# Top-8 search over five interleaved segments instead of six contiguous ones, in a top-k attention and MLP kernel

## The chip, the cores and the metric

The kernel runs on one core of one Trainium2 chip. The core has five engines that work side by side and meet only through semaphores: TensorE (PE in the profile, with its weight loads as PEld), VectorE (DVE), ScalarE (ACT), GpSimd (POOL) and SyncE (SP), which issues most of the DMAs. The metric is the device time of one execution in microseconds (us), the median of several runs.

## What is computed

Sparse attention for 8 batches of 8 heads, 576 tokens, head size 64: each row of scores keeps only its 32 largest of 576 values, and a softmax over those weights the values. The result, 4608 tokens of 512 features, goes through a two-layer MLP with a leaky ReLU whose slope is given per hidden unit.

```python
scores = scale * np.matmul(q, k.transpose(0, 1, 3, 2))
kth = np.partition(scores, -top_k, axis=-1)[..., -top_k:-top_k + 1]     # top_k = 32
scores = np.where(scores >= kth, scores, -1000000000.0)
attn = np.exp(scores - np.max(scores, axis=-1, keepdims=True))
attn = attn / (np.sum(attn, axis=-1, keepdims=True) + 1e-09)
x = np.matmul(attn, v)                       # 8 x 8 x 576 x 64, then heads side by side
...
h = x @ w_in                                 # 512 -> 2048
g = np.maximum(h, 0.0) + alpha * np.minimum(h, 0.0)
return g @ w_out                             # 2048 -> 512
```

## The kernel before

**Tiles.** Two heads form a pair; there are 32 pairs. A tile is 128 rows of scores, 576 wide; a pair has nine, of which the ninth holds the 64 rows left over from each of its two heads. That makes 288 tiles of [128, 576].

**How the 32nd value is found.** For each row a threshold is guessed from the mean and the spread of its scores (`prep_plan`, once per pair: small matmuls on PE, `P` on DVE, then a short chain of DVE operations to `NT0`). ACT subtracts it: `b` is score minus guess. ACT then sums the signs of `b` into `S_all`, which tells how many of the row's scores lie above the guess, and so on which side the wanted value lies and how many places away. POOL makes the side into a sign bit, `SG`. DVE flips bits of `b` by it (`flip`, the tile `y`), so that the values on the wanted side nearest to the guess become the largest. Now only the 24 largest of `y` are needed, in order.

- `seg_ops` cuts the 576 values of `y` into NSEG segments and takes the eight largest of each with one DVE instruction (`nc.vector.max`, MAX8 in the profile). The results stand side by side in `C`, 8 NSEG values a row.
- `merge_ops` takes the 24 largest of those in three rounds into `L`: MAX8 over all of `C`, then a match-and-replace that strikes the eight out (two instructions in the profile, MATCH_VALUE_LOAD and MATCH_REPLACE8), twice over.
- `sel_a` (ACT), `sel_eq`, `sel_pr` and `sel_sum` (DVE, for three tiles at a time) pick the wanted one of the 24 into `KK`; `limit` turns it back into a limit `KP` for `b`.
- `check_group` keeps, once per nine tiles, the largest eighth value of any segment in `M8`. If a row's wanted value lies below it, one segment may have held more than eight candidates. At the end `checks` counts over all rows that this and three other conditions hold; if any fails, a flag sends the whole kernel through a slow second path (`general_batch`).

**After the limit.** DVE makes a 0/1 mask `mk` (`mask`), ACT the exponentials `e` for two tiles at once, POOL multiplies both into `w` (`weights`). A DMA transposes `w` to `wT`. PE multiplies it with the values into `pu` (`av`), which has a column of ones for the sum; DVE takes the reciprocal `rz`, ACT scales into `xb`. Further DMA transposes give `xT`, and PE and ACT run the MLP on it in blocks (`ph`, `gT`, `pz`, `o_sb`), with the second term of the leaky ReLU folded into the weights beforehand.

**What sets the order.** The order on each engine is written out by hand: the main loop goes through ticks n, and in each of them issues

- on PE the scores of the next unit of one or two tiles (two PSUM buffers), a slice of the MLP or of the weights' preparation, then the steps of `prep_plan` and `av` due in this tick;
- on ACT the evacuations left over from the tick before (`gT`, `o_sb`), then `b`, the sign sum and `e` of tile n, then what is due;
- on DVE first the mask of tile n - 7, then the search of tile n - 2 and the merge of tile n - 3, one instruction of each in turn, then what is due (the limits, the steps of `prep_plan`), then the flip of tile n - 1;
- on POOL first `w` of tile n - 7, which waits for the mask of this tick, then `SG` of tile n - 1, for which the flip at the end of this tick waits.

Each engine works through its own list in order, so an instruction that waits holds everything behind it on that engine. `b` has five buffers of two tiles, `e` four, `y` two, `C` two of nine tiles each. `P` is read by PE, and DVE reads its PSUM source from a pool of two banks that `pu` uses as well.

The lines to follow are 369 (the search), 384 and 386 (the merge), 359 (`y`), 433 (`mk`), 443 (`w`), 353 (`SG`), 246 (`P`), 337, 343 and 348 (`b`, the sign sum, `e`), 328 (scores), 494 (`pu`), 697, 703 and 715 (the MLP). The turn of search and merge in one tick is this:

```python
segs = seg_ops(n - LAG_S) if 0 <= n - LAG_S < NT else []
...
for i in range(max(len(segs), len(merges), 2)):
    if i < len(segs):
        segs[i]()
    if i < len(merges):
        merges[i]()
```

Of the kernel before, what the change touches and what calls it, by code (L numbers as in the profile page):

```python
# [14 lines left out]
PS = bass.MemoryType.PSUM  # L15

S = 576
NSEG = 6
SEG = S // NSEG
KW = 24  # L20
TINY = 1.0e-30
ZSQ = 0.640625
# [10 lines left out]
def kernel(  # L33
# [10 lines left out]
    nc = tc.nc  # L44
# [8 lines left out]
    TPP = 9  # L53
# [109 lines left out]
    n = 0  # L163
# [200 lines left out]
    def seg_ops(n):  # L364
        if n % TPP == 0:
            Cs[n // TPP] = prep.tile([128, TPP, NSEG, 8], FP32, name="C", bufs=2)
        C = Cs[n // TPP]
        t = tiles[n]
        return [lambda g=g: nc.vector.max(out=C[:, n % TPP, g, :],  # L369
                                          in_=t["y"][:, g * SEG:(g + 1) * SEG])  # L370
                for g in range(NSEG)]

    Ls, sel, KPs = {}, {}, {}

    def merge_ops(n):
# [3 lines left out]
        L = Ls[n // 3][:, n % 3, :]  # L379
        C2 = attn.tile([128, NSEG * 8], FP32, name="C2", bufs=1)  # L380
        ops = []
# [368 lines left out]
    with tc.manual_schedule(engines={E.PE, E.Activation, E.DVE, E.Pool, E.SP}):  # L750
# [84 lines left out]
        n = 0  # L835
        end = max(NT + 24, 0)
        while n < end or back or after:
# [55 lines left out]
            if 0 <= n - 1 < NT:  # L893
                side_of(n - 1)
            segs = seg_ops(n - LAG_S) if 0 <= n - LAG_S < NT else []
            mn = n - LAG_M
            merges = merge_ops(mn) if 0 <= mn < NT else []
# [167 lines left out]
```

## Time and profile before

| | us |
|---|---|
| median of 3 runs | 874.53 |
| lowest and highest run | 871.5, 876.87 |
| the profiled execution | 873.98 |
| its span, first to last instruction | 872.1 |
| mean granted TensorE clock in it | 0.943 |

The costliest groups of DVE and ACT, by line, operation, output and input (partitions x elements), count, then busy time and mean nanoseconds of one, then idle time of the engine just before them and what ended it:

```profile
L384 DVE MAX8 L<-C 128x8 f32<-128x48 f32 x864 | 162.6, 188 | 0.1
L359 DVE TENSOR_SCALAR y<-b,SG 128x576 int32<-128x576 int32 x288 | 147.0, 510 | 8.2 <-POOL SG L353 7.8
L433 DVE TENSOR_SCALAR mk<-b,KP 128x576 bf16<-128x576 f32 x282 | 143.6, 509 | 0.0
L386 DVE MATCH_REPLACE8 C<-L,C 128x48 f32<-128x48 f32 x576 | 108.3, 188 | 0.0
L337 ACT ACTIVATE b<-ps,NT 128x576 f32<-128x576 f32 x288 | 202.3, 761 | 3.1 <-PE ps L328 3.1
L343 ACT ACTIVATE h<-b 128x576 bf16<-128x576 f32 x288 | 202.9, 705 | 1.7
```

Successive instructions of one engine overlap in such a profile: the drawn time of one reaches into the next, so busy time of a group is more than the time it takes on its engine. The chain of waits gives each piece only the time by which it carries the chain on. Times in a trace count from the span's start.

### The profile page before, as it was taken

The numbers are of one execution on the slowest core, as the hardware profiler recorded it, in microseconds if no ns is written. First come the engines' busy times: TensorE is split into PE (matmuls) and PEld (weight loads), VectorE is DVE, ScalarE is ACT, GpSimd is POOL, SyncE is SP. The second block draws the span as 40 slices with busy tenths as digits, with TensorE's granted clock in tenths as the row PEclk, the third lists the DMA queues.
The fourth block names the chain that finished last, engine by engine and source line by source line (L and its number), as shares of the span: only waits on it lengthen the run. The fifth ranks groups of instructions, "written<-read, shape, count | busy, mean of one in ns | idle before, by whom it ended". The sixth has DMA issues, their size and how long they took to land.

```text
span 872.1 us, 20608 instructions
## 1 busy us (share of the span) xinstructions
PE 721.9 (83%) x5697; PEld 428.3 (49%) x5771; DVE 835.1 (96%) x5188; ACT 790.3 (91%) x1873; POOL 431.0 (49%) x630
## 2 busy tenths in 40 slices
PE   6776688778978789787987789977897988899996
PEld 4443444334554345444454445643455554566674
DVE  4999999999999999999999999999999999999992
ACT  6999999999999999889999999989999899979861
POOL 1455545555454555545555455554554555544530
PEclk9997779899979999989998999989999999999999
DMA  7999644644665545564576445475455543535442
GB/s 161 156 178 199 131 89 90 126 91 97 135 139 107 108 102 116 100 135 95 114 154 115 98 97 116 111 136 98 92 128 121 121 103 81 106 71 100 91 96 56
DMA packets 342619, 99.37 MB, mean 114 GB/s; under 512 B 334672, under 2 KB 334944, under 8 KB 342496
## 3 DMA queue, kind: packets, MB, share of 16 engines
q1 hardware_dynamic: 340144, 95.58, 54.4%
q0 software_dynamic: 1152, 2.10, 2.0%
q8 instruction: 47, 0.77, 0.4%
q14 instruction: 76, 0.62, 0.2%
q10 hardware_dynamic: 1200, 0.30, 0.2%
HBM read 36.71 MB, written 9.44 MB: 53 GB/s over the span
## 4 chain that ended last, share of the span: by engine, by line
DVE 62%; ACT 21%; PE 12%; DMA 2%; issue 1%; POOL 1%; SPq 0%; DVEq 0%; another core or an unknown queue 0%; ACTq 0%
DVE C L369 20%; DVE y L359 9%; DVE mk L433 9%; DVE C L386 8%; DVE L L384 7%; ACT b L337 5%; ACT h L343 5%; ACT e L348 4%; PE ps L328 4%; PE pz L715 3%; PE ph L697 2%; ACT gT L703 2%; DVE P L246 2%; ACT xb L523 2%; PE pu L494 1%
## 5 line engine op out<-in xcount | busy, mean ns | idle before, releaser
L443 POOL TENSOR_TENSOR w<-mk,e 128x576 bf16<-128x576 bf16 x250 | 319.3, 1277 | 337.9 <-DVE mk L433 187.5
L369 DVE MAX8 C<-y 128x8 f32<-128x96 f32 x1728 | 419.1, 243 | 0.1
L328 PE MATMUL ps<-qkT 64*128 64x288 f32 (+1 forms) x1280 | 256.5, 474 | 35.1 <-ACT b L337 34.6
L337 ACT ACTIVATE b<-ps,NT 128x576 f32<-128x576 f32 x288 | 202.3, 761 | 3.1 <-PE ps L328 3.1
L343 ACT ACTIVATE h<-b 128x576 bf16<-128x576 f32 x288 | 202.9, 705 | 1.7
L697 PE MATMUL ph<-xT,w_in_b 128*128 128x128 bf16 (+2 forms) x997 | 150.4, 292 | 40.8 <-ACT gT L703 33.6
L328 PEld LDWEIGHTS ps<-qkT 64*128 64x128 f32 (+1 forms) x1280 | 134.3, 194 | 97.6 <-ACT b L337 59.8
L348 ACT ACTIVATE e<-b 128x1152 bf16<-128x1152 f32 (+1 forms) x158 | 174.2, 1102 | 0.0
L384 DVE MAX8 L<-C 128x8 f32<-128x48 f32 x864 | 162.6, 188 | 0.1
L359 DVE TENSOR_SCALAR y<-b,SG 128x576 int32<-128x576 int32 x288 | 147.0, 510 | 8.2 <-POOL SG L353 7.8
L433 DVE TENSOR_SCALAR mk<-b,KP 128x576 bf16<-128x576 f32 x282 | 143.6, 509 | 0.0
L715 PE MATMUL pz<-w_out_b,gT 128*128 128x512 bf16 x543 | 132.4, 380 | 1.2 <-issue 0.5
L697 PEld LDWEIGHTS <-w_in_b 128*128 128x128 bf16 x1024 | 80.4, 100 | 104.0 <-issue 79.6
L703 ACT ACTIVATE gT<-ph 128x512 bf16<-128x512 f32 x140 | 86.0, 621 | 28.1 <-PE ph L697 28.1
L386 DVE MATCH_REPLACE8 C<-L,C 128x48 f32<-128x48 f32 x576 | 108.3, 188 | 0.0
L715 PEld LDWEIGHTS <-gT 128*128 128x128 bf16 x560 | 51.6, 98 | 68.5 <-issue 14.0
L494 PE MATMUL pu<-v_bf,wT 128*128 128x65 bf16 (+1 forms) x1600 | 69.4, 198 | 14.4 <-DMA wT<-w 6.9
L494 PEld LDWEIGHTS <-wT 128*128 128x128 bf16 (+1 forms) x1600 | 65.2, 103 | 25.6 <-issue 10.2
L353 POOL TENSOR_SCALAR SG<-S_all 128x1 int32<-128x1 f32 x288 | 65.3, 227 | 18.9 <-ACT h L343 18.8
L443 POOL TENSOR_TENSOR wm<-mk,e 128x576 bf16<-128x576 bf16 x32 | 40.8, 1276 | 49.9 <-DVE mk L433 45.6
L343 ACT ACTIVATION_READ_ACCUMULATOR h<-b 128x1 f32 x288 | 62.8, 218 | 0.0
L523 ACT ACTIVATE xb<-pu,rz 128x64 bf16<-128x64 f32 x224 | 54.5, 369 | 0.0
(113 smaller groups left out, 728.1 us busy)
## 6 DMA issues: line engine op xcount, KB each, us to landing
out_dram<-o_sb SPq DMA_DIRECT2D x34, 256.0 KB, 2.3
st_q<-in_q_dram SPq DMA_DIRECT2D x64, 128.0 KB, 2.8
st_v<-in_v_dram SPq DMA_DIRECT2D x64, 128.0 KB, 2.6
kst<-in_k_dram SPq DMA_DIRECT2D x62, 128.0 KB, 2.6
w_stage<-in_moe_w_out_dram SPq DMA_DIRECT2D x16, 256.0 KB, 3.1
w_in_b<-in_moe_w_in_dram POOLq DMA_DIRECT2D x8, 256.0 KB, 6.4
wT<-w SPq DMA_TRANSPOSE x128, 3.3
st_q<-in_q_dram SPq DMA_DIRECT2D x32, 32.0 KB, 2.5
```

Of the source, the lines that this page charges most:

```text
L328: nc.tensor.matmul(o_, l_, r_, start=True, stop=True)
L337: nc.scalar.activation(t["b"].rearrange("p (a c) -> p a c", a=2), t["ps"], AF.Identity, bias=NT0[:, p * TPP + j:p * TPP + j + 1], scale=ON ...
L343: nc.scalar.activation(h, tiles[n]["b"], AF.Sign, accum_out=S_all[:, n:n + 1])
L348: nc.scalar.activation(e, tiles[n0]["bu"], AF.Exp, scale=scl)
L359: nc.vector.tensor_scalar(t["y"].bitcast(I32), t["b"].bitcast(I32), FLIP, SG[:, n:n + 1], ALU.bitwise_xor, ALU.bitwise_xor)
L369: return [lambda g=g: nc.vector.max(out=C[:, n % TPP, g, :], in_=t["y"][:, g * SEG:(g + 1) * SEG]) for g in range(NSEG)]
L384: ops.append(lambda r=r, src=src: nc.vector.max(out=L[:, 8 * r:8 * r + 8], in_=src))
L386: ops.append(lambda r=r, src=src: nc.vector.match_replace(out=C2, in_to_replace=L[:, 8 * r:8 * r + 8], in_values=src, imm_value=NEG))
L433: nc.vector.tensor_scalar(t["mk"], t["b"], row_limit(n), None, ALU.is_ge)
L443: nc.gpsimd.tensor_tensor(dst, t["mk"], t["e"], ALU.mult)
L697: nc.tensor.matmul(hold[f][:, i, :], w_in_b[:, kk, (f + i) * 128:(f + i + 1) * 128], xT[:, kk, c0:c0 + tb], start=(kk == 0), stop=(kk == N ...
L715: nc.tensor.matmul(pz[0:m], hold["gT"][:, f, r0:r0 + m], w_out_b[:, f, :], start=False, stop=(f == NFT - 1))
```

## The change

The six segments of 96 neighbouring values become five. The 576 values of a row are taken as 72 runs of eight neighbours, and segment g is made of the runs g, g + 5, g + 10 and so on: segments 0 and 1 have 15 runs (120 values), segments 2, 3 and 4 have 14 (112 values). One MAX8 reads each segment, with an access pattern of runs of eight words 40 words apart. `C` holds 40 values a row instead of 48, and the merge, the check and the small tile that the merge works in follow from NSEG. All lines below the constants move up by one, and the search stays on line 369.

```diff
 S = 576
-NSEG = 6
-SEG = S // NSEG
+NSEG = 5
 KW = 24
...
         t = tiles[n]
-        return [lambda g=g: nc.vector.max(out=C[:, n % TPP, g, :],
-                                          in_=t["y"][:, g * SEG:(g + 1) * SEG])
+        y = t["y"].rearrange("p (t e) -> p t e", e=8)
+        return [lambda g=g: nc.vector.max(out=C[:, n % TPP, g, :], in_=y[:, g:S // 8:NSEG, :])
                 for g in range(NSEG)]
```

## The prediction

> **What bounds the kernel now.** I read the page first, then the chain of waits in order of time, then the table of stretches cut where that chain changes engine.
>
> ```profile
> PE 721.9 (83%) x5697; PEld 428.3 (49%) x5771; DVE 835.1 (96%) x5188; ACT 790.3 (91%) x1873; POOL 431.0 (49%) x630
> DVE 62%; ACT 21%; PE 12%; DMA 2%; issue 1%; POOL 1%; SPq 0%; DVEq 0%; another core or an unknown queue 0%; ACTq 0%
> ```
>
> The change acts on DVE, which is 96% busy and holds 62% of the chain. But ACT is 91% busy: the average says only that two engines are close. So I look at where the chain lies on DVE.
>
> ```profile
> 118.37 0.82 DVE P L246 x2
> ...
> 351.19 1.24 PE pu L494 x30
> ...
> 427.98 0.81 DVE P L246 x2
> ...
> 811.66 0.49 DVE y L359
> ...
> 854.57 0.19 PE ptot L481 x2
> ```
>
> From 118 to 351 us the chain is DVE alone, from 351 to 428 ACT and PE, from 428 to 646 DVE again, then ACT and PE until 812, and DVE until 855. Before 118 it changes hands often.
>
> ```profile
> 40.00:118.00 78.00, 54.58 (x335) 32.69 (x341) 75.22 (x472) 76.06 (x174) 42.69 (x61) 0.80 0.87 160
> 118.00:351.00 233.00, 193.74 (x1494) 109.30 (x1513) 232.63 (x1450) 222.47 (x542) 121.36 (x171) 0.95 0.55 110
> 428.00:646.00 218.00, 183.56 (x1450) 104.36 (x1472) 218.00 (x1360) 205.31 (x505) 113.74 (x160) 0.96 0.56 115
> ...
> 812.00:855.00 43.00, 42.20 (x463) 28.73 (x464) 42.39 (x235) 29.99 (x59) 16.17 (x22) 1.00 0.47 94
> ```
>
> The columns are stretch, length, then busy time of PE, weight load, DVE, ACT, POOL. In both long DVE stretches DVE has no gap (232.63 of 233.00; 218.00 of 218.00), and ACT is idle for 10.5 and 12.7 us. What matters is whether that idle time is ACT waiting for DVE, which would shrink with DVE, or something else.
>
> ```profile
> PE ph L697 <- ACT gT L703: 10.5, 15, 1.5
> ...
> PE pu L494 <- DVE P L246: 5.1, 5, 1.9
> ```
>
> These are PE's own waits from 118 to 352 us. The same view from 428 to 646 us has:
>
> ```profile
> PE pu L494 <- DVE P L246: 1.0, 1, 1.0
> ```
>
> And ACT's waits over the whole run:
>
> ```profile
> ACT gT L703 <- PE ph L697: 28.1, 30, 2.6
> ACT o_sb L720 <- PE pz L715: 25.8, 15, 4.6
> ```
>
> ACT waits for PE and PE for ACT; ACT's list names DVE nowhere. The only door by which DVE holds the pair back is PE waiting for a PSUM bank that DVE's P product still reads: 5.1 us in the first long stretch (1.9 of it the single wait at 351 us that the chain goes through), 1.0 us in the second. So ACT and PE are a closed loop that is nearly as slow as DVE by itself.
>
> **The change, part by part.** The price of one search instruction is its place in the chain, not its drawn length, since neighbours overlap.
>
> ```profile
> 641.72 0.17 DVE C L369
> 641.88 0.11 DVE L L384
> 641.99 0.15 DVE C L369
> 642.14 0.18 DVE C L386
> ...
> 643.20 0.16 DVE C L369
> ```
>
> One tile runs six such C searches of 96 elements (0.16 us each on average), three L searches of 48 (0.11) and two match-and-replace pairs of 48 (0.18). It goes from 641.72 to 643.36, 1.64 us. From 96 to 48 elements the place shrinks by 0.05 us, 1.04 ns an element, so a fixed 0.06 us is left per instruction.
>
> (1) Five segments, two of 120 and three of 112 elements, still read 576 elements together; one fixed part goes: -0.06 us per tile. (2) The three L searches and two replacements read 40 instead of 48 elements: 5 x 8 x 1.04 ns = -0.04 us. The two value loads stay. (3) The check over the eighth of each segment reads 45 instead of 54 elements, 32 times: 0.3 us in all, left out. No DMA, no queue entry and no wait on another engine is added or moved. The five searches and five merge steps alternate as before, one search between dependent merge steps; only the search behind the last L search is gone, and what reads L next comes after y. Sum: -0.10 us per tile, 288 tiles, 30 us of DVE work.
>
> (4) The new cost is the way of reading: runs of eight words, then a jump of 40. No search in the trace reads so. The nearest rows:
>
> ```profile
> L407 DVE TENSOR_REDUCE KK<-L 128x3 f32<-128x72 f32 x96 | 20.7, 216 | 0.1
> L461 DVE TENSOR_REDUCE M<-C 128x9 f32<-128x54 f32 x32 | 7.5, 235 | 0.0
> ```
>
> L407 reads 72 adjacent words, so at 1.04 ns its fixed part is 141 ns. L461 picks every eighth word: (235 - 141) / 54 = 1.74 ns an element, 0.70 more than an adjacent one. If only the first word after a jump pays, 72 x 0.70 ns = 0.05 us per tile and half the saving is gone; if every word pays, 576 x 0.70 = 0.40 us and DVE loses 0.30 per tile; if a jump is free, nothing. A gain I exclude: the words are as many and none is read faster than in turn. I take nothing, since seven of eight words follow their neighbour as in L407, and keep 0 to 0.05 for the range. [...]
>
> (5) What DVE then waits for. In each pass y needs SG from POOL, and POOL does SG behind w, which needs this pass's mask mk.
>
> ```profile
> 403.10 0.51 DVE L433 TENSOR_SCALAR mk<-b,KP 128x576 bf16<-128x576 f32 x1
> 403.70 1.27 POOL L443 TENSOR_TENSOR w<-mk,e 128x576 bf16<-128x576 bf16 x1 [2.09 <-DVE mk L433]
> 404.94 0.23 POOL L353 TENSOR_SCALAR SG<-S_all 128x1 int32<-128x1 f32 x1
> 405.02 0.24 DVE L369 MAX8 C<-y 128x8 f32<-128x96 f32 x1
> 405.20 0.52 DVE L359 TENSOR_SCALAR y<-b,SG 128x576 int32<-128x576 int32 x1
> ```
>
> SG ends at 405.17, y starts at 405.20: in this pass there is no slack, although no wait is drawn (the search's drawn end covers it). The pass in the middle of nine later ones:
>
> ```profile
> 520.18 0.23 POOL L353 TENSOR_SCALAR SG<-S_all 128x1 int32<-128x1 f32 x1
> ...
> 520.70 0.51 DVE L359 TENSOR_SCALAR y<-b,SG 128x576 int32<-128x576 int32 x1
> ```
>
> Here y comes 0.29 us after SG's end. Read so over the nine passes from 515.11 to 537.90 us, three have 0.03 to 0.05 us between SG's end and y, six have 0.14 to 0.95. So of 9 x 0.10 us only about 6 x 0.10 passes through: 0.07 us per tile while DVE sets the pace.
>
> **The sum, stretch by stretch.** The searches of each stretch, six a tile:
>
> ```profile
> 40.00:118.00 78.00, 39.15 (x161) 0.80 0.87 160
> 118.00:351.00 233.00, 118.02 (x486) 0.95 0.55 110
> 428.00:646.00 218.00, 110.33 (x456) 0.96 0.56 115
> 812.00:855.00 43.00, 17.64 (x72) 1.00 0.47 94
> ```
>
> Before 118: 27 tiles, but ACT is busy 76.06 of 78.00, so between nothing and 27 x 0.07 = 1.9; I take -0.7, as DVE holds 47 of these 118 us of the chain (62% of 872 less the three later stretches' 494). First long stretch: DVE would shed 81 x 0.07 = 5.7, but ACT and PE follow at once when PE's waits for DVE are used up: at least the 1.9 at 351 us, at most 5.1; middle 3.5. 351 to 428: nothing, ACT and PE. Second: DVE sheds 76 x 0.07 = 5.3, PE's wait is only 1.0; -0.5 (0 to 1.0). 646 to 812: nothing; the pair sets it, and an earlier DVE only waits longer for S_all. 812 to 855: twelve tiles, 0.8 on DVE, but PE is busy 42.20 of 43.00, so at most that; -0.6. Together -5.3, and between -2 and -9 at the ends. The profiled execution took 873.98 us (span 872.1, 1.9 around it; the median of the runs is 874.53): 873.98 - 5.3 = 868.7, with 865 to 872 for this case alone.
>
> **The rivals.**
>
> (A) ACT's idle time gives way too, so that DVE's gain comes through in all its stretches: (27 + 81 + 76 + 12) x 0.07 = 13.7: 860. Without the POOL limit, at 0.10, it would be 854. For it: ACT's 23 us of idle in those stretches is room enough. Against: that idle ends on PE, not on DVE.
>
> (B) Nothing comes of it: jumps cost 0.05 us per tile, which leaves 0.05, and the pair takes over after 2 us: 872, up to 875 with what runs scatter.
>
> (C) Slower by the way of reading: every word pays as in L461, DVE loses 0.30 us per tile in 288 tiles, and DVE sets the pace everywhere: 874 + 86 = 960. It decides from about 0.20 ns an element, where (4) eats the 0.10. Against: seven words of eight follow their neighbour. [...]
>
> (D) Slower by PE's clock: with ACT and PE setting the pace, PE's pauses move:
>
> ```profile
> 367.78 1.87 PE L697 MATMUL ph<-xT,w_in_b 128*128 128x512 bf16 x4 [2.19 <-DMA xT<-xb]
> 370.12 3.13 PE L328 MATMUL ps<-qkT 64*128 64x288 f32 x8
> ...
> 377.46 1.24 PE L328 MATMUL ps<-qkT 64*128 64x288 f32 x8
> ```
>
> After a pause of 2.19 us eight score products take 3.13 instead of 1.24: with the ph group, about 4 us are lost. Four more such pauses without a gain elsewhere would make 890. Fewer would add 4 each to the gain. [...]
>
> (E) The kernel does more than the change says: if one row has eight of the values ahead of its wanted one in a single segment, the flag sends the whole kernel through its slow second path, which alone adds over a millisecond of searches (320 tiles of 576 elements, seven passes at 0.66 us from the prices above). Worked out on the reference's inputs by the kernel's formulas, the wanted rank is at most 18 and no row has more than seven there.
>
> **How the numbers follow.** My forecast 0.50, A 0.30, B 0.10, C 0.04, D 0.05, E 0.01. About 1% is what a measurement of this kernel tells from no change; faster is below 865.8, 1% under the median. A lies there, and a fifth of the forecast's chance for a pair with a little more room: 0.40. The rest of the forecast and B stay within 1%: 0.50. C, D and E are slower: 0.10. The range for 8 in 10 leaves out C, D, E and A's end at 854: from 857 to 876.
>
> **What would show it.**
>
> ```profile
> L369 DVE MAX8 C<-y 128x8 f32<-128x96 f32 x1728 | 419.1, 243 | 0.1
> ```
>
> This group becomes x1440 at a mean of 243 + 19 x 1.04 = 263 ns; above 270 a jump has a price, near 343 it is C (115 x 0.70 more). L searches and replacements get 8 ns shorter. In the two long stretches DVE's busy share falls below 99% with waits of y on SG and of P on PE, and "PE pu <- DVE P" all but goes; the chain there turns to ACT and PE. If DVE is still without a gap and the time is near 860, the step that gave ACT and PE no room was wrong. If C searches cost as forecast and the time doesn't move, the pair was the bound before as well.

## The result, and the profile after

| | before | after |
|---|---|---|
| median of 14 runs each, us | 874.0 | 870.01 |
| lowest and highest run, us | 871.35, 877.89 | 866.45, 875.27 |
| profiled execution, us | 873.98 | 871.45 |
| its span, us | 872.1 | 869.6 |

The ratio after to before is 0.9959 [0.9943, 0.9976] (in brackets the 95% interval): faster by 4.0 us, and within 1%. The forecast was 868.7, in a range from 857 to 876.

The page of the changed kernel, busy time by engine and then the chain that ended last:

```profile
PE 714.7 (82%) x5697; PEld 424.1 (49%) x5771; DVE 814.2 (94%) x4900; ACT 789.5 (91%) x1873; POOL 431.1 (50%) x630
...
PE 15%; ACT 10%; DVE 1%; issue 0%; POOL 0%; DVEq 0%
```

DVE gave up 288 instructions and 20.9 us of drawn time; ACT did the same work as before. The chain could be followed back only over the last quarter of the span (the shares add to 26%), so of the long stretches it says nothing. For those, here is the table of stretches (length, then busy time of PE, weight load, DVE, ACT and POOL, then granted clock, DMA share and GB/s):

```profile
40.00:118.00 78.00, 50.17 (x328) 29.36 (x331) 71.37 (x429) 74.39 (x170) 40.85 (x59) 0.71 0.87 153
118.00:351.00 233.00, 193.40 (x1522) 109.49 (x1546) 231.24 (x1400) 222.35 (x544) 124.34 (x175) 0.96 0.57 114
...
428.00:646.00 218.00, 184.94 (x1464) 105.34 (x1483) 212.70 (x1290) 204.93 (x504) 114.49 (x161) 0.95 0.59 114
```

DVE now has gaps: 1.8 us in the first long stretch and 5.3 in the second, where it had 0.4 and none. The groups of DVE, shapes kept apart:

```profile
L369 DVE MAX8 C<-y 128x8 f32<-128x112 f32 x864 | 225.2, 261 | 0.0
L383 DVE MAX8 L<-C 128x8 f32<-128x40 f32 x864 | 155.7, 180 | 0.1
L369 DVE MAX8 C<-y 128x8 f32<-128x120 f32 x576 | 154.9, 269 | 0.1
L358 DVE TENSOR_SCALAR y<-b,SG 128x576 int32<-128x576 int32 x288 | 147.4, 512 | 11.2 <-POOL SG L352 8.6
...
L385 DVE MATCH_REPLACE8 C<-L,C 128x40 f32<-128x40 f32 x576 | 103.8, 180 | 0.0
L385 DVE MATCH_VALUE_LOAD C<-L,C 128x8 f32 x576 | 39.9, 69 | 0.1
L245 DVE TENSOR_TENSOR P<-pr,qkT 128x512 bf16<-128x512 f32 x32 | 22.0, 687 | 12.2 <-PE pr L237 12.0
```

The 1440 searches take (225.2 + 154.9) / 1440 = 264 ns each; 263 was forecast for free jumps, and L searches and replacements went from 188 to 180. The new idle time is that of P, which waits 12.0 us for PE (2.7 before). On PE's side, the waits of the whole run:

```profile
PE ph L696 <- ACT gT L702: 38.4, 51, 1.5
PE ps L327 <- ACT b L336: 36.5, 32, 2.9
PE pt L215 <- ACT qkT L211: 26.0, 26, 2.4
PE pu L493 <- DMA wT<-w: 11.1, 2, 5.7
```

PE waiting for P's bank, the door of the prediction, is in this list nowhere any more. PE waits for ACT, and DVE for PE.

What a tile costs is best read from the starts of y, once a tile. A pair has nine tiles, so that y's tenth start, less the first, is the time of one pair. In the timeline of before:

```profile
560.77 0.52 DVE L359 TENSOR_SCALAR y<-b,SG 128x576 int32<-128x576 int32 x1
...
586.42 0.52 DVE L359 TENSOR_SCALAR y<-b,SG 128x576 int32<-128x576 int32 x1
```

And of after, the same nine places in a pair, with all ten starts:

```profile
325.93 0.52 DVE L358 TENSOR_SCALAR y<-b,SG 128x576 int32<-128x576 int32 x1
328.62 0.50 DVE L358 TENSOR_SCALAR y<-b,SG 128x576 int32<-128x576 int32 x1
331.37 0.50 DVE L358 TENSOR_SCALAR y<-b,SG 128x576 int32<-128x576 int32 x1
333.98 0.50 DVE L358 TENSOR_SCALAR y<-b,SG 128x576 int32<-128x576 int32 x1
336.73 0.50 DVE L358 TENSOR_SCALAR y<-b,SG 128x576 int32<-128x576 int32 x1
339.74 0.52 DVE L358 TENSOR_SCALAR y<-b,SG 128x576 int32<-128x576 int32 x1
342.33 0.52 DVE L358 TENSOR_SCALAR y<-b,SG 128x576 int32<-128x576 int32 x1
344.88 0.52 DVE L358 TENSOR_SCALAR y<-b,SG 128x576 int32<-128x576 int32 x1
348.43 0.51 DVE L358 TENSOR_SCALAR y<-b,SG 128x576 int32<-128x576 int32 x1
350.96 0.52 DVE L358 TENSOR_SCALAR y<-b,SG 128x576 int32<-128x576 int32 x1
```

25.65 us before, 25.03 after: 0.62 less for nine tiles, 0.069 a tile. That is the pair when DVE waits for nothing. Not every pair is one: of the 24 pairs between tile 36 and tile 252 the median is 25.66 before and 25.31 after, because P then waits for PE (12 times, 12.0 us). Where the two traces drift apart is seen from the start of y for single tiles, after less before:

| tile | before, us | after, us | after - before |
|---|---|---|---|
| 27 | 94.10 | 97.97 | +3.87 |
| 36 | 121.71 | 123.12 | +1.41 |
| 117 | 353.78 | 350.96 | -2.82 |
| 126 | 379.43 | 376.00 | -3.43 |
| 144 | 431.30 | 429.13 | -2.17 |
| 198 | 586.42 | 582.49 | -3.93 |
| 216 | 637.72 | 635.77 | -1.95 |
| 279 | 819.99 | 818.01 | -1.98 |
| 287 | 842.47 | 839.86 | -2.61 |

Nearly 4 us are lost up to tile 27, of which 2.5 are made good by tile 36. The first long stretch makes the rest good and gains, and in the second the gain is won and lost again.

### The profile page after: what moved, and what is told of

Same layout as the page of the kernel before. It is cut to its first block, busy times and chain, and to the rows that moved or that the text cites. A ratio compares the mean times of both kernels' runs of the same rounds, so it can differ in the third digit from the quotient of the medians.

```text
span 869.6 us, 20320 instructions
## 1 busy us (share of the span) xinstructions
PE 714.7 (82%) x5697; PEld 424.1 (49%) x5771; DVE 814.2 (94%) x4900; ACT 789.5 (91%) x1873; POOL 431.1 (50%) x630
## 5 line engine op out<-in xcount | busy, mean ns | idle before, releaser
L369 DVE MAX8 C<-y 128x8 f32<-128x112 f32 (+1 forms) x1440 | 380.0, 264 | 0.1
L327 PE MATMUL ps<-qkT 64*128 64x288 f32 (+1 forms) x1280 | 252.8, 467 | 36.9 <-ACT b L336 36.5
L696 PE MATMUL ph<-xT,w_in_b 128*128 128x128 bf16 (+2 forms) x997 | 151.2, 293 | 41.6 <-ACT gT L702 38.4
L327 PEld LDWEIGHTS ps<-qkT 64*128 64x128 f32 (+1 forms) x1280 | 131.2, 190 | 97.7 <-ACT b L336 60.8
L358 DVE TENSOR_SCALAR y<-b,SG 128x576 int32<-128x576 int32 x288 | 147.4, 512 | 11.2 <-POOL SG L352 8.6
L383 DVE MAX8 L<-C 128x8 f32<-128x40 f32 x864 | 155.7, 180 | 0.1
L702 ACT ACTIVATE gT<-ph 128x512 bf16<-128x512 f32 x140 | 85.9, 621 | 26.4 <-PE ph L696 26.2
L385 DVE MATCH_REPLACE8 C<-L,C 128x40 f32<-128x40 f32 x576 | 103.8, 180 | 0.0
L352 POOL TENSOR_SCALAR SG<-S_all 128x1 int32<-128x1 f32 x288 | 65.2, 227 | 22.0 <-ACT h L342 21.8
```

The costliest lines, as they stand in the source:

```text
L327: nc.tensor.matmul(o_, l_, r_, start=True, stop=True)
L358: nc.vector.tensor_scalar(t["y"].bitcast(I32), t["b"].bitcast(I32), FLIP, SG[:, n:n + 1], ALU.bitwise_xor, ALU.bitwise_xor)
L369: return [lambda g=g: nc.vector.max(out=C[:, n % TPP, g, :], in_=y[:, g:S // 8:NSEG, :]) for g in range(NSEG)]
L383: ops.append(lambda r=r, src=src: nc.vector.max(out=L[:, 8 * r:8 * r + 8], in_=src))
L696: nc.tensor.matmul(hold[f][:, i, :], w_in_b[:, kk, (f + i) * 128:(f + i + 1) * 128], xT[:, kk, c0:c0 + tb], start=(kk == 0), stop=(kk == N ...
```

## The experiments

The theory, from the prediction: the search as changed is cheaper by 0.10 us a tile, jumps are free, POOL's loop from mask to sign holds three of nine passes, and the time follows little because ACT and PE are nearly as slow by themselves. The rivals: the jumps cost what the saved instruction gave; the POOL loop is the limit; or no second limit is there, and the gain is only small.

### Do the jumps cost anything?

Six segments again, but of runs of eight with jumps of 48 words: one line of the changed kernel is edited, and against before nothing but the way of reading differs:

```diff
-NSEG = 5
+NSEG = 6
```

> Six segments again, but read as runs of eight words with jumps of 48 (the new way of reading alone, 96 elements as before). Theory (jumps are free): the search's mean stays at 243 ns within 2, and the time is that of the kernel before, ratio 0.998 to 1.002. Rival (jumps have a price that ate part of the saving): at 0.70 ns for the first word after each jump the search's mean is 251 ns, DVE loses 0.05 us per tile where it sets the pace, and the time is 8 to 14 us above the kernel before.

Measured: 873.95, ratio 1.0006 [0.9986, 1.0026]. The groups:

```profile
L369 DVE MAX8 C<-y 128x8 f32<-128x96 f32 x1728 | 426.2, 247 | 0.1
L383 DVE MAX8 L<-C 128x8 f32<-128x48 f32 x864 | 166.3, 192 | 0.1
```

The search is drawn 4 ns longer than before's 243, more than I had allowed. But the L search, whose reading isn't changed, is drawn 4 ns longer too (192 for 188): searches and merges are drawn some 2% longer in this profile. Drawn lengths move so without any jump too: in a later kernel with before's own search (the square on POOL, below) the two are drawn at 240 and 186. The place in the queue decides, and nine passes take 25.64 us (y at 560.71 and 586.35), as before, where a price of 0.05 us a tile would have made 0.45 more. These jumps cost nothing that shows here.

The other way round, five segments of neighbours, with the widths of the changed kernel (the edit is shown against that kernel):

```diff
+CUT = [0, 120, 240, 352, 464, 576]
...
-        y = t["y"].rearrange("p (t e) -> p t e", e=8)
-        return [lambda g=g: nc.vector.max(out=C[:, n % TPP, g, :], in_=y[:, g:S // 8:NSEG, :])
+        return [lambda g=g: nc.vector.max(out=C[:, n % TPP, g, :],
+                                          in_=t["y"][:, CUT[g]:CUT[g + 1]])
```

> Five segments of neighbours (120, 120, 112, 112, 112 values): the change without its jumps. Theory: the same lengths as in the changed kernel (mean 264 ns) and the same time, 868 to 872, ratio about 0.996. Rival (jumps have a price): the mean is 8 to 11 ns shorter and DVE has more room; since ACT and PE set the pace the time would still gain little, so the length of the search tells these apart, not the time.

Measured: 870.37, ratio 0.9968 [0.9948, 0.9988], the changed kernel's within the interval.

```profile
L369 DVE MAX8 C<-y 128x8 f32<-128x112 f32 x864 | 228.0, 264 | 0.0
...
L369 DVE MAX8 C<-y 128x8 f32<-128x120 f32 x576 | 156.6, 272 | 0.1
```

Neighbours are drawn no shorter than runs with jumps (261 and 269 in the changed kernel), and a quick pair takes 25.02 us. For the time it is the number of segments that counts; interleaving does nothing (870.37 without it, 870.01 with it).

### Does the time follow DVE any further down?

Four segments (the count in the flag's test is set so that it never strikes):

```diff
-NSEG = 5
+NSEG = 4
...
-        nc.vector.tensor_scalar(bad, pt, float(128 * NT * 4) - 0.5, None, ALU.is_lt)
+        nc.vector.tensor_scalar(bad, pt, -0.5, None, ALU.is_lt)
```

> Four segments of 144 values, merged from 32; the final check's flag is never raised (that decision is left out, the check's own work stays). DVE sheds another 0.10 us of work per tile. Theory (since the change ACT and PE set the pace): 867 to 871, at most 2 us below the changed kernel, and DVE's waits for PE and POOL grow by about what it sheds, some 20 us. Rival (DVE still sets the pace in the changed kernel): as much again as the change was to bring with DVE as the only bound, 0.07 us in each of some 200 tiles, so 856 or less.

Measured: 870.51, ratio 0.9954 [0.9937, 0.9972]. The time is that of the theory, but this run shows nothing, since DVE was not made quicker: nine passes take 25.15 us at best. The reason stands in the merge's group:

```profile
L383 DVE MAX8 L<-C 128x8 f32<-128x32 f32 x864 | 157.9, 183 | 10.0
```

10.0 us of idle time before the L searches, 0.1 in the changed kernel. Four searches no longer stand between all of the five merge steps, and the last L search, which needs the replacement just ahead of it, waits for it with nothing between:

```profile
411.68 0.17 DVE L385 MATCH_REPLACE8 C<-L,C 128x32 f32<-128x32 f32 x1
411.88 0.20 DVE L383 MAX8 L<-C 128x8 f32<-128x32 f32 x1
```

From the start of that replacement to the next instruction it is 0.20 us; with a search between, in the changed kernel, it is 0.10. That 0.10 a tile is what four segments in place of five were to save.

So the search was cut without touching the merge: five segments, but they read only the first half of each row (and the flag never strikes, as above). What this kernel leaves out is the candidates in the second half.

```diff
-        return [lambda g=g: nc.vector.max(out=C[:, n % TPP, g, :], in_=y[:, g:S // 8:NSEG, :])
+        return [lambda g=g: nc.vector.max(out=C[:, n % TPP, g, :], in_=y[:, g:S // 16:NSEG, :])
```

> The changed kernel with its five searches reading only the first half of each row (288 of 576 values, five searches of 56 or 64); the second half of the candidates is left out, and the final check's flag is never raised. Unlike with four segments, the five searches still stand between the merge steps. DVE's own work falls by 288 x 1.04 ns = 0.30 us per tile, but POOL's loop (mask, w, SG, y) floors a pass: nine passes should go from 25.0 to about 24.4 us where nothing else waits. Theory (ACT and PE set the pace of the changed kernel): 866 to 871, less than 4 us below it, and DVE waits 10 us or more longer for PE and POOL. Rival (DVE, with POOL's loop, still sets the pace): 0.07 us per tile more is gained, 15 us, 856 or less.

Measured: 870.31, ratio 0.9957 [0.9941, 0.9974]: no quicker than the changed kernel, with 288 x 288 elements less to read, 86 us of DVE work at 1.04 ns. DVE's waits over the whole run, and the long stretches:

```profile
DVE y L358 <- POOL SG L352: 32.4, 104, 3.3
DVE P L245 <- PE pr L237: 22.8, 19, 2.6
```

```profile
118.00:351.00 233.00, 195.85 (x1544) 110.23 (x1543) 217.03 (x1396) 221.30 (x541) 124.06 (x174) 0.95 0.57 113
428.00:646.00 218.00, 187.82 (x1485) 106.68 (x1483) 201.92 (x1302) 208.22 (x511) 115.84 (x163) 0.95 0.59 116
```

DVE stands idle for 16 us in each long stretch, and ACT is busy as before. What the search gives up now turns into waits for POOL and PE. Something else sets the pace, and the changed kernel stands already at the point where it does. POOL's loop is not enough to explain it: seven of the 27 pairs from tile 36 on take 24.50 to 24.52 us, so the loop allows that, and still the 27 together take 693.3 us, against 694.9 in the changed kernel.

In the other direction, the kernel before with a seventh, short search:

```diff
-                for g in range(NSEG)]
+                for g in range(NSEG)] + [lambda: nc.vector.max(out=spare, in_=t["y"][:, 0:40])]
```

> The kernel before with one more search per tile, of 40 values into a tile that nobody reads: 0.06 + 0.04 = 0.10 us more on DVE per tile, the size of what the change takes off. Theory (DVE set the pace of the kernel before almost from end to end, with ACT and PE just behind): adding costs nearly in full, 0.10 us in some 230 to 288 tiles, 895 to 902, five times what taking off the same brought. Rival (ACT and PE were the bound before the change too, DVE merely full beside them): less than 8 us, below 882.

Measured: 895.18, ratio 1.0244 [1.0216, 1.0272]. Nine passes take 26.50 us (0.85 more, 0.094 a tile), DVE has no gap in the long stretches (233.00 of 233.00, 218.00 of 218.00), it holds 78% of the chain, and the door opens wide:

```profile
PE pu L495 <- DVE P L246: 19.1, 13, 2.9
```

0.09 us a tile added cost 21 us; 0.07 to 0.10 taken off gave 4. On the side of more work DVE decides (21 us are 0.073 for each of 288 tiles); on the side of less it doesn't.

### Is it POOL's loop?

The sign of tile n - 1 ahead of w in POOL's list, in the changed kernel:

```diff
             held = []
+            if 0 <= n - 1 < NT:
+                side_of(n - 1)
             for wn in due:
...
-            if 0 <= n - 1 < NT:
-                side_of(n - 1)
```

> The changed kernel with POOL doing SG ahead of w in each pass, so that y no longer waits behind the mask and w. Theory: the three passes of nine that kept their length (2.53, 2.59 and 3.01 us) get 0.05 to 0.10 us shorter, the quickest nine passes go from 25.0 to about 24.7 us, which shows that POOL's loop held them; the time stays within 868 to 873, since ACT and PE set the pace. Rival (those passes were held by something else): nine passes stay at 25.0.

Measured: 870.99, ratio 0.9953 [0.9931, 0.9975]. The three passes that kept their length under the change (3.01, 2.59 and 2.53 us) now take 2.92, 2.47 and 2.41, and the quickest pair takes 24.66 in place of 25.03. So POOL's loop did hold them, and the time is the same 870 with the loop open.

But the edit has a price of its own. In POOL's list w now stands behind a sign that waits for ACT, 207.8 us here and 21.8 in the changed kernel:

```profile
L352 POOL TENSOR_SCALAR SG<-S_all 128x1 int32<-128x1 f32 x288 | 90.0, 313 | 208.6 <-ACT h L342 207.8 <-DMA wT<-w 0.5
```

Where w comes late by that, it meets DVE's EQ or y, and these then last until w is done:

```profile
211.97 0.23 POOL L352 TENSOR_SCALAR SG<-S_all 128x1 int32<-128x1 f32 x1 [2.40 <-ACT h L342]
...
212.16 1.28 POOL L442 TENSOR_TENSOR w<-mk,e 128x576 bf16<-128x576 bf16 x1
...
212.52 1.01 DVE L396 TENSOR_TENSOR EQ<-ra,iota 128x72 f32<-128x72 f32 x1
```

In this profile 15 of the 96 EQ overlap w and take 723 ns in the mean (210 where POOL does nothing), and 13 y overlap it and take 947 (511). So this run alone doesn't tell what an open loop is worth; together with the half search, which left POOL's list as it was, it speaks against the loop as what sets the time. That POOL waits 207.8 us for ACT already points to ACT.

### Is it ACT?

If ACT and PE set the pace, then with less on ACT the change should be worth more. Two steps were moved from ACT to POOL, each in both kernels. First the cast of the values, for all pairs from the third on:

```diff
+        def pool_v():
+            nc.gpsimd.tensor_copy(d["v"][:, :, 0:D], d["st_v"])
...
-            ts = [-14, -13, -12, -11, -10, -9, -7, -6, -5, -5, -4, -4, -3, -2, -8]
+            ts = [-14, -13, -12, -11, -10, -9, -7, -6, -5, -5, -4, -4, -3, -2, -9]
...
-                 dict(dve=[dve_6]), dict(act=[act_v])]
+                 dict(dve=[dve_6]),
+                 dict(act=[act_v]) if p < 2 else dict(pool=[pool_v])]
...
                 side_of(n - 1)
+            run(n, "pool")
```

> The kernel before with one step taken off ACT: the cast of a pair's values to bf16 (0.73 us drawn, 30 of 32 pairs) goes to POOL's idle time behind SG in the pass with the most slack. ACT sheds about 19 us. Theory (DVE set the pace before): nine passes of DVE stay at 25.65 and the time falls by at most 4 us, 870 to 874. Rival (ACT was the bound before as well): 860 or less.

> The same step taken off ACT in the changed kernel. Theory (ACT and PE set the pace now, and DVE could do nine passes in 25.0 us): the pair's floor falls below DVE's, DVE runs without gaps from about 120 to 740 us, some 10 us are gained: 857 to 864, so that the change is worth 9 us or more with ACT relieved, against 4 without. Rival (PE, not ACT, is what DVE now waits for): 867 to 871.

Measured: before 884.62, ratio 1.0116 [1.0087, 1.0145]; after 870.46, ratio 0.996 [0.9945, 0.9976]. Both missed their forecasts (870 to 874 and 857 to 864), and the second lies where its rival said, 867 to 871, though not for the rival's reason. The cause is a collision that I had not thought of, in the timeline of the second:

```profile
528.58 0.72 POOL L205 CAST v_bf<-st_v 128x640 bf16<-128x640 f32 x1
...
528.62 0.69 DVE L246 TENSOR_TENSOR km<-GK,bones 128x2 bf16<-128x2 bf16 x1
```

km, a product of two elements a partition, ends with POOL's cast, 0.69 us after its start. Over the run it takes 584 ns in this kernel and 142 in the changed one. So each pair costs DVE half a microsecond more: nine passes take 26.10 us with six segments and 25.58 with five. In both DVE has next to no gap left (218.00 and 217.51 of 218.00 in the second long stretch). The same change is worth 884.62 - 870.46 = 14.2 us here. But that doesn't show what it was meant to: DVE was made dearer in both, and on that side of the balance DVE decides without any relief of ACT, as the seventh search showed. This pair of runs leaves open whether ACT holds the changed kernel.

Then the square in front of the selection (`sel_a`), two short instructions on POOL (0.3 us the longer); POOL has the signs and these ahead of w:

```diff
-        nc.scalar.activation(a, S_all[:, 3 * m:3 * m + 3], AF.Square, bias=c513)
+        nc.gpsimd.tensor_scalar(a, S_all[:, 3 * m:3 * m + 3], 513.0, 1.0, ALU.add, ALU.mult)
+        nc.gpsimd.tensor_tensor(a, a, a, ALU.mult)
...
             run(n, "act")
-            if n >= 3 and n % 3 == 0 and n - 3 < NT:
-                sel_a((n - 3) // 3)
...
             held = []
+            if 0 <= n - 1 < NT:
+                side_of(n - 1)
+            if n >= 3 and n % 3 == 0 and n - 3 < NT:
+                sel_a((n - 3) // 3)
             for wn in due:
...
-            if 0 <= n - 1 < NT:
-                side_of(n - 1)
```

> The kernel before with another step taken off ACT, one that does not meet DVE on POOL: the square of S_all + 513 for three tiles (96 of them, 0.32 us drawn, 0.19 of ACT's time each, 18 us in all) becomes two small POOL operations, and POOL does SG and these ahead of w in each pass. Theory (DVE sets the pace of the kernel before): nine passes stay at 25.65 us and the time falls by 0 to 4 us, 870 to 874. Rival (ACT was the bound before the change): 862 or less.

> The same two edits in the changed kernel. DVE can do nine passes in 24.7 us once POOL's loop is open. Theory (ACT's work holds the changed kernel): with 18 us off ACT the pair's floor sinks and 5 to 12 us are gained against the changed kernel, 858 to 865; the change is then worth 8 us or more instead of 4. Rival (PE, not ACT, sets the floor of the pair): 868 to 871, as with SG ahead of w alone.

Measured: before 871.39, ratio 0.9971 [0.9958, 0.9984]; after 860.18, ratio 0.9841 [0.9821, 0.9862]. With ACT relieved of 96 squares, the change is worth 11.2 us, and here DVE was not made dearer: the kernel with six segments keeps its 25.60 us a pair. The chain and the long stretches of the second:

```profile
DVE 47%; PE 23%; ACT 23%; DMA 3%; issue 3%; POOL 1%; SPq 0%; ACTq 0%; DVEq 0%; POOLq 0%
```

```profile
118.00:351.00 233.00, 197.74 (x1530) 110.60 (x1553) 232.76 (x1403) 219.28 (x516) 146.97 (x232) 0.93 0.59 114
428.00:646.00 218.00, 185.44 (x1487) 106.49 (x1506) 217.99 (x1331) 209.27 (x498) 141.84 (x219) 0.98 0.61 118
```

DVE is without a gap again, although a pair takes it only 24.90 us in the median of the same 24 pairs (25.60 with the square on POOL and six segments). This kernel is quicker than both, by 14.3 us against before's 874.45 beside it, and by 9.8 against after's 870.01. Against the kernel with the sign first alone (870.99), which differs only by the squares, these are worth 10.8 us, or 9.8 by the ratios to before (0.9953 and 0.9841). So 96 ACT instructions, drawn at 0.32 us each and together 13.4 us of ACT's busy time (789.5 to 776.1), count, while 86 us of DVE work did not. ACT is shown by this as what held the changed kernel. That PE, on which ACT waits in turn, holds it as well is read from the waits alone; no run takes work off PE.

Both steps off ACT together, the sign first, and the cast behind w, one tick earlier (-10), so that it meets no km:

> The changed kernel with both steps off ACT (the square and the cast of the values, 37 us of ACT in all), SG first, and the cast behind w one pass earlier than in the run before, in a pass without the products km and P on DVE. Theory: with ACT well clear DVE sets the pace at 24.7 to 25.2 us for nine passes: 853 to 862. If the cast holds y or another DVE operation as it held km (0.69 instead of 0.14 us), nine passes take 25.3 or more and the time is 862 to 870.

Measured: 858.98, ratio 0.9835 [0.9815, 0.9855], within the forecast, but it can't be told from the kernel with the square alone. DVE's `EQ` shows why, here and then in the changed kernel:

```profile
L401 DVE TENSOR_TENSOR EQ<-ra,iota 128x72 f32<-128x72 f32 x96 | 31.4, 327 | 0.0
```

```profile
L396 DVE TENSOR_TENSOR EQ<-ra,iota 128x72 f32<-128x72 f32 x96 | 19.9, 207 | 0.0
```

The cast no longer meets km, but now it meets EQ: 25 of the 96 overlap it and take 618 ns in the mean, some 200 where POOL does nothing. (With the square alone the mean of all is 234, some of it held by w.) What ACT sheds, DVE pays: the median pair takes 25.10 us, 24.90 with the square alone.

## Why the prediction was right, point by point

**The saving (1, 2): right.** In the places of a pair that wait for nothing, passes went from 2.78, 2.85, 2.74, 2.85 and 2.65 us to 2.69, 2.75, 2.61, 2.75 and 2.55, and the long pass of P from 3.65 to 3.55: 0.10 us in the mean, as summed.

**The way of reading (4): right.** Nothing for jumps between runs of eight words, shown twice: 25.64 us for nine passes with jumps and 25.65 without, then 25.03 with and 25.02 without. The price worked out from L461 for a jump at every word holds as well: the check over every eighth word (M) went from 235 to 219 ns with nine elements less, 1.8 ns each. Rivals B and C fall: B had nearly the right time (872) for a reason that is not there. (C would have decided from 0.17 ns an element, 0.10 us over 576, and not from 0.20; nothing hangs on it.)

**POOL's loop (5): right.** The passes that end on the sign stayed at 3.01, 2.59 and 2.53 (3.02, 2.59 and 2.53 before) while the six others shrank, so 0.62 us a pair came through of 0.9. No wait shows it: DVE's waits for SG were 7.8 us before and are 8.6 after. The loop was found from the distance between SG's drawn end and y's start, and the run with the sign first confirms it: just these passes got shorter. That waits of y for SG would show in the long stretches was wrong for the same reason.

**The pair ACT and PE takes over: right, shown for ACT, argued for PE.** Taking DVE work away does nothing more, adding it costs at once, and taking 96 squares from ACT lets the change through to 11 us. Rival A was right that there was that much to be had in DVE's stretches, and wrong in its reason that ACT's idle time was room enough. The reading that fits is that ACT and PE, which wait for each other in turn, show idle time on both and have none to give (in the changed kernel PE waits 38.4 us for ACT's gT, and that gT 26.2 us for PE's ph). Even with ACT relieved not all comes through: 0.10 us for the 162 tiles from 45 to 207 would be 16 us, and the two kernels with the square on POOL draw apart by 11.4 there.

**The sum by stretches: total near, single terms off.** By the table of y starts:

| stretch | forecast, us | profile, us |
|---|---|---|
| before 118 (to tile 36) | -0.7 | +1.4 |
| 118 to 351 (36 to 117) | -3.5 | -4.2 |
| 351 to 428 (117 to 144) | 0 | +0.7 |
| 428 to 646 (144 to 216) | -0.5 | +0.2 |
| 646 to 812 (216 to 279) | 0 | 0.0 |
| 812 to the end (279 to 287) | -0.6 | -0.6 |
| sum | -5.3 | -2.6 |

The spans differ by 2.5, the medians by 4.0; a single pair of profiles can't settle a microsecond. That 5.3 comes so near to 4.0 is in part luck: four of the six terms are off by 0.7 us or more, and not all to one side. The largest miss is the first term. "Between nothing and 1.9" left a loss out: the terms were bounded by what DVE and ACT shed, and transfers were taken as unmoved. In that stretch PE waits once, near 80 us, for a transpose of w, 4.2 us before and 5.7 after, with the DMA engines busy for 0.87 of the stretch in both. Tile 13 is late by 1.6 us ahead of this wait already, tile 22 by 2.9 behind it, tile 27 by 3.9. That the change does this is not shown: this one wait is 2.6 to 6.3 us in the profiles of the five kernels with six or seven searches and 4.5 to 7.0 in those of the eight others. From the first y to tile 27 the four kernels with six searches take 79.2 to 81.9 us and the eight with five or four 81.1 to 84.6, so it leans that way, with less DVE work in each of the eight. Nor is it PE's clock: the kernel with six interleaved segments had 0.77 and 0.65 in the first two stretches (1.00 and 0.80 before, 0.76 and 0.71 after) and its tile 27 came at 93.44, ahead of before's. The cause of the loss stays open.

**What was to show in the profile.** The search at 264 ns (263), L and replacement 8 ns shorter, PE's waits for P gone: as forecast. DVE's share under 99% came true in the second long stretch (97.6%), not quite in the first (99.2%). P waits for PE as forecast. The chain lies on PE and ACT as far as it reaches, but that is only from 636 us on, so for the long stretches this sign was not seen.

**Rival D** happened on a small scale, for and against, and didn't decide (below). **Rival E** did not happen: DVE has just the 288 searches less, and nothing more.

## What to carry to other kernels

Where two engines are both over 90% busy, ask what the second takes when the first waits for nothing: adding 0.09 us a tile to DVE cost 21 us, taking 0.10 away gave 4, and 11 appeared only when the second engine was relieved too. A row with next to no idle time (8.2 us before 288 y) can hide a loop with no slack: compare the drawn end of what an instruction needs with its start, pass by pass. A relief that makes the first engine dearer, as the cast on POOL did (26.10 us for nine passes in place of 25.65), tests nothing. And a merge whose steps depend on each other needed other work between them here: with one search fewer than merge steps, the saving came back as a stall (0.20 us in place of 0.10 from the replacement's start to the next instruction).

## What the runs showed of the hardware

**Some DVE instructions are drawn longer beside POOL's.** In the pass where km met a POOL cast of 128x640 from f32 to bf16 (0.72 us), it took 0.69 us in place of 0.14, and the EQ that met the cast took 618 ns in the mean in place of some 200. With POOL's product w (1.28 us in that list) it was the same in the run with the sign first: EQ that overlapped it took 723 ns in the mean, y 947 in place of 511. In the lists of before and after w is over when y starts, since y waits for the sign behind w. The searches meet w in every pass and show next to nothing of it: between 100 and 800 us of before they are drawn at 0.24 us beside w, and at 0.23 in the 18 that met nothing on POOL. In the two lists above km ends 0.01 us after the cast, and EQ 0.09 us after w. The opening has the engines meet only through semaphores. These lengths don't fit that for POOL and DVE; what makes them longer, the traces don't show.

**The same pause, another clock.** After, and then before, in PE's timeline:

```profile
190.90 1.97 PE L327 MATMUL ps<-qkT 64*128 64x288 f32 x6 [1.73 <-ACT b L336]
```

```profile
190.11 1.23 PE L328 MATMUL ps<-qkT 64*128 64x288 f32 x6 [1.74 <-ACT b L337]
```

The same six products at the same place, behind the same pause (1.73 and 1.74 us), take 1.97 in one execution and 1.23 in the other; the granted clock is 0.59 over the first (190.9 to 192.9) and 1.00 over the second. ACT's gT then waits 2.33 us for PE in the first and 0.75 in the second. The slow products of rival D came again in part: before, behind the pause of 2.19 us for xT, the clock is 0.51 from 367.0 to 377.5; after, behind a pause of 2.39 us for ACT at 364.3, it is 0.69 from 366.0 to 370.5 and then 1.00. So the length of the pause alone doesn't tell the clock behind it, and what does is not shown. In this one case gT waits 1.6 us longer, as much as the terms of the sum by stretches.

**Drawn lengths differ between profiles.** The 96-element search was drawn at 240, 243 and 247 ns in three kernels, and the merge's search at 186, 188 and 192, while nine passes took 25.60, 25.65 and 25.64 us. Lengths should be compared within one profile, or by the starts of what comes once a pass.
